# Spreading the cluster products and output transposes of the first pairs of heads over more steps, in a fused clustered-attention and channel-mix kernel

## The chip, the cores and the metric

The kernel runs on one core of a Trainium2 chip. The metric is the device time of one execution, in microseconds (us). The kernel before the change takes 252.67 us, the median of three runs (252.64 to 252.88). The profiled execution has a span of 250.9 us from its first to its last instruction, and all times read from the profile count from the start of that span.

The engines are named as in the profile: PE is the matrix engine (PEld its weight loads), DVE the vector engine, ACT the scalar engine, POOL the GpSimd engine, SP the engine that here issues most of the DMAs.

## The reference

Attention in which a query sees only the keys of its own cluster, and then a channel mix on its output:

```python
# q, k, v: (4, 8, 768, 64) f32; centroids: (8, 16, 64); d_model 512, d_ff 1024
q_assign = argmax(einsum('bhsd,hcd->bhsc', q_n, c_n), -1)      # unit-length q, centroids
k_assign = argmax(einsum('bhsd,hcd->bhsc', k_n, c_n), -1)
mask = q_assign[:, :, :, None] == k_assign[:, :, None, :]
attn = softmax(where(mask, q @ k.T / sqrt(64), -1e9))
x = (attn @ v), heads joined to (4, 768, 512)
x_prev = x shifted by one position
xk = mu_k * x + (1 - mu_k) * x_prev;  xr = mu_r * x + (1 - mu_r) * x_prev
out = sigmoid(xr @ w_r) * (relu(xk @ w_k) ** 2 @ w_v)
```

## The kernel before

The four batches of eight heads are 16 pairs of heads, numbered 0 to 15. The program is written by hand as a sequence of steps, numbered `t`; a head has six steps, a pair twelve, all heads 192. In each step the PE computes one block of scores (128 keys by 768 queries), the ACT takes its exponential, and the PE multiplies an earlier head's block with its values. The mask costs no step of its own: the 16 rows under the 64 rows of q and of k hold the one-hot code of the cluster (`aug`), so that one product of 80 rows gives score and mask at once.

```python
def scores(t):                        # one step: two matmuls and one exponential
    ...
    st = ps_st.tile([128, S], F32, name="st")          # ps_st has two buffers
    nc.tensor.matmul(st[:, 0:512], kc, a[rows, 0:512], start=True, stop=True)
    nc.tensor.matmul(st[:, 512:S], kc, a[rows, 512:S], start=True, stop=True)
    nc.scalar.activation(pt, st, AF.Exp, bias=-BIG, scale=BIG)
```

What stands between the steps prepares a coming pair: 12 transposes of its q and k on the PE (`more`, two a step for pairs 2 to 5, with a DVE copy of each four and a cast into `aug` on POOL), the product with the cluster centroids (`aff_mm`), the choice of the largest and the transposition of the one-hot code on the DVE (`aff_max`, `aff_back`), and four small DMAs that carry the code into rows 64 to 79 of `aug`.

```python
def aff_mm(n, part=0, parts=1):       # columns of one part, four products of them
    if part == 0:
        aff[n] = ps_w.tile([128, GW], F32, name="affps", tag="w")   # ps_w has two buffers
    u = slice(part * GW // parts, (part + 1) * GW // parts)         # GW = 384
    for g in range(NG):
        nc.tensor.matmul(ps[32 * g:32 * g + 32, u], cblk[...], qkT[n][:, g, u], ...)
    if part == parts - 1:
        nc.vector.transpose(t1, ps)

def aff_back(n, engs):
    nc.vector.transpose(oht, ohns[n % 2])
    for i, g in enumerate((0, 2, 1, 3)):               # the first head's two, then the second's
        engs[i % len(engs)].dma_start(augs[n % NR][g % 2][64:64 + C, ...], oht[32 * g:32 * g + C, :])
```

The output of a pair is turned by six PE transposes and one DVE copy (`xtr`), from which the two mixtures `xk` (`shift`) and `xr` (`shift_r`) are made on the DVE. The products with `w_k`, `w_r` and `w_v` of the first batch (`psk`, `psr`, `psv`) start at step 58.

The first pair goes another way, with smaller pieces (`first_trans`, `first_aff`, `first_onehot`), so that the first scores come early. The start and the steps that the change touches:

```python
nc.scalar.dma_start(cn_sb, centroids.rearrange("h c d -> (h c) d"))
nc.scalar.preload_act_table(AF.Sqrt)
load_head(0, nc.sync, nc.scalar)      # q on SP's queue, k on ACT's queue
load_head(1, nc.sync, nc.scalar)
...
cnt_ps = ...; nc.tensor.transpose(cnt_ps..., cn_sb, ident); two copies into cblk   # centroids
first_trans(0, 0); first_trans(0, 1)
use_pe(4)                             # four matmuls on zeros
first_trans(1, 0); first_aff(0, 0); first_aff(0, 1); first_trans(1, 1); first_aff(1, 0)
... first_onehot(0); first_aff(1, 1)

def first_onehot(t):                  # per head: 6 transposes of q, 6 of k, a copy of each
    for i in range(2):
        ps = ps_w.tile([128, S], BF16, name="ohps", tag="w")
        ... if i == 0: nc.vector.tensor_copy(dst, ...)
            else: nc.scalar.copy(dst, ...)
```

In a step the order on the PE is: scores, values (in every sixth step last), the step's `forced` piece, and then what `at` has put there. [...]

The softmax here doesn't subtract the row's maximum and nothing guards it: scores larger than these inputs give would overflow.

## Time and profile before

| What | Before |
|---|---|
| device time, median of 3 | 252.67 us |
| span of the profiled execution | 250.9 us |
| PE busy | 238.7 us, 95% |
| ACT busy | 189.4 us, 75% |
| DVE busy | 176.6 us, 70% |
| first score matmul starts at | 10.87 us |
| exponentials on ACT | 192, of 811 ns each |

How to read it: "busy" is the union of the times of an engine's instructions. A wait is put down to whatever ended last before it. The chain of waits follows the last instruction back in time; the timeline lists the instructions of an engine, and merges equal ones ("x4") that follow each other without a pause, with the idle time before them in square brackets. A share of the whole span hides that the kernel has several stages with different limits, so the stages are read one by one.

### The profile page before, as it was taken

To read this page: it belongs to the slowest core of one execution; us is meant where nothing else is said; L and a number is where in the kernel's file an instruction comes from. 1 tells how busy PE (TensorE), PEld (TensorE's weight loads), DVE (VectorE), ACT (ScalarE), POOL (GpSimd) and SP (SyncE) were. 2 spreads that over 40 slices of the span, in tenths; PEclk is the share of its full clock that TensorE was granted. 3 is DMA by queue.
4 is the path that set the end of the run, shared out by engine and by line. 5 is a ranking of instruction groups with operands and counts; after the bars stand their busy time and mean duration, and the time that the engine had idled before them with its cause. 6 is when DMAs were issued, how large, how long until landed. Compare 5 with 4: busy or idle time off the path is not lost.

```text
span 250.9 us, 6203 instructions
## 1 busy us (share of the span) xinstructions
PE 238.7 (95%) x2364; PEld 146.5 (58%) x2395; DVE 176.6 (70%) x340; ACT 189.4 (75%) x271; POOL 106.0 (42%) x190
## 2 busy tenths in 40 slices
PE   8999989998998999999999999999999998899994
PEld 3866766765665555555676555556566555355442
DVE  3576778698899994979967778679844427865222
ACT  5398988999897977878999877878899785146210
POOL 2968848571999737080827153712801000000000
PEclk9999999999999999999999999999999999999999
DMA  6995897879978586965959689794121121110122
GB/s 176 260 258 94 153 280 143 112 140 168 178 114 170 92 176 127 201 123 120 206 67 157 80 185 131 167 163 152 34 79 29 47 70 48 56 72 0 70 98 86
DMA packets 102462, 31.87 MB, mean 127 GB/s; under 512 B 74721, under 2 KB 98977, under 8 KB 102433
## 3 DMA queue, kind: packets, MB, share of 16 engines
q1 hardware_dynamic: 98352, 27.97, 54.3%
q0 software_dynamic: 2208, 2.62, 7.0%
q10 hardware_dynamic: 1872, 0.89, 1.3%
q8 instruction: 19, 0.31, 0.5%
q14 instruction: 11, 0.08, 0.1%
HBM read 24.15 MB, written 6.29 MB: 121 GB/s over the span
## 4 chain that ended last, share of the span: by engine, by line
PE 75%; DVE 10%; ACT 8%; issue 2%; DMA 2%; SPq 0%; DVEq 0%; ACTq 0%
PE psv L405 15%; PE st L286 13%; PE out L299 10%; PE psk L382 10%; PE psr L394 7%; ACT pt L289 7%; PE st L287 6%; PE psk L373 5%; PE affps L194 4%; DMA aug<-oht 2%; PE wps L463 2%; DVE xr L358 2%; DVE k L388 1%; DVE oht L217 1%; DVE xk L358 1%
## 5 line engine op out<-in xcount | busy, mean ns | idle before, releaser
L289 ACT ACTIVATE pt<-st 128x768 bf16<-128x768 f32 x192 | 148.2, 811 | 23.2 <-PE st L287 22.8
L175 POOL TENSOR_SCALAR aug<-qkT 64x384 bf16<-64x384 f32 x128 | 74.8, 584 | 73.1 <-DVE qkT L145 52.2
L286 PE MATMUL st<-aug 80*128 80x512 bf16 x192 | 73.1, 381 | 2.5 <-ACT pt L289 1.0
L299 PEld LDWEIGHTS <-pt 128*128 128x128 bf16 x1152 | 59.9, 97 | 26.6 <-ACT pt L289 1.4
L299 PE MATMUL out<-vt,pt 128*128 128x65 bf16 x1152 | 66.0, 193 | 0.9 <-ACT pt L289 0.8
L287 PE MATMUL st<-aug 80*128 80x256 bf16 x192 | 51.9, 270 | 0.0
L405 PE MATMUL psv<-w_v_sb,k 128*128 128x512 bf16 x173 | 44.5, 378 | 1.4 <-ACT tanh L397 0.7
L387 ACT ACTIVATE kr<-psk 128x512 bf16<-128x512 f32 x48 | 28.8, 601 | 8.1 <-PE psk L382 5.6
L388 DVE TENSOR_TENSOR k<-kr 128x512 bf16<-128x512 bf16 x48 | 22.4, 473 | 17.0 <-ACT kr L387 16.9
L382 PE MATMUL psk<-xk,w_k_sb 128*128 128x512 bf16 x113 | 30.6, 378 | 1.5 <-DVE t L198 0.8
L412 DVE SCALAR_TENSOR_TENSOR out_sb<-tanh,psv 128x512 f32<-128x512 bf16 x23 | 15.7, 682 | 21.7 <-PE psv L405 17.8
L286 PEld LDWEIGHTS <-aug 80*128 80x128 bf16 x192 | 18.7, 97 | 17.3 <-issue 7.8
L397 ACT ACTIVATE tanh<-psr 128x512 bf16<-128x512 f32 x24 | 14.4, 599 | 19.1 <-PE psr L394 18.5
L405 PEld LDWEIGHTS <-k 128*128 128x128 bf16 x184 | 16.1, 97 | 16.4 <-issue 2.4
L287 PEld LDWEIGHTS <-aug 80*128 80x128 bf16 x192 | 18.9, 98 | 9.7 <-issue 1.6
L394 PE MATMUL psr<-w_r_sb,xr 128*128 128x512 bf16 x91 | 23.7, 378 | 0.2
L145 DVE STREAM_TRANSPOSE qkT<-qk_nat 128x384 f32<-128x384 f32 x40 | 21.5, 557 | 0.0
L182 POOL CAST vt<-v_nat 128x384 bf16<-128x384 f32 x32 | 17.0, 560 | 9.5 <-DMA v_nat<-in_v_dram 8.7
L312 DVE TENSOR_TENSOR xn<-out,rs 128x384 bf16<-128x384 f32 x32 | 17.8, 558 | 1.1
L198 DVE STREAM_TRANSPOSE t<-affps 128x384 f32<-128x384 f32 x15 | 8.7, 580 | 14.0 <-PE affps L194 13.9
L382 PEld LDWEIGHTS <-w_k_sb 128*128 128x128 bf16 x128 | 11.2, 97 | 10.2 <-issue 0.9
L358 DVE SCALAR_TENSOR_TENSOR xk<-diff,mu_k_sb,xt 128x768 bf16<-128x768 bf16 x16 | 16.7, 1043 | 0.6
(65 smaller groups left out, 206.2 us busy)
## 6 DMA issues: line engine op xcount, KB each, us to landing
v_nat<-in_v_dram SPq DMA_DIRECT2D x16, 384.0 KB, 4.2
out_dram<-out_sb SPq DMA_DIRECT2D x23, 256.0 KB, 2.8
qk_nat<-in_q_dram SPq DMA_DIRECT2D x40, 96.0 KB, 4.3
qk_nat<-in_k_dram SPq DMA_DIRECT2D x40, 96.0 KB, 3.6
qk_rows<-in_q_dram SPq DMA_DIRECT2D x5, 384.0 KB, 4.4
qk_rows<-in_k_dram SPq DMA_DIRECT2D x4, 384.0 KB, 5.3
aug<-oht SPq DMA_DIRECT2D x60, 24.0 KB, 2.0
w_k_sb<-in_moe_w_k_dram POOLq DMA_DIRECT2D x4, 256.0 KB, 5.6
```

What stands on the lines that cost most here:

```text
L145: nc.vector.transpose(qkT[n][:, g, :], nat[n][:, g // 2, (g % 2) * GW:(g % 2 + 1) * GW])
L175: nc.gpsimd.tensor_scalar(augv(n, g)[0:64, par, :], in0=qkT[n][64 * par:64 * par + 64, g, :], scalar1=qk_scale, scalar2=1.0, op0=ALU.mult, ...
L286: nc.tensor.matmul(st[:, 0:512], kc, a[rows, 0:512], start=True, stop=True)
L287: nc.tensor.matmul(st[:, 512:S], kc, a[rows, 512:S], start=True, stop=True)
L289: nc.scalar.activation(pt, st, AF.Exp, bias=-BIG, scale=BIG)
L299: nc.tensor.matmul(o[:, (qc + NCH // 2) % NCH, :], pts[bh * NCH + c][:, qc * 128:(qc + 1) * 128], vts[n % NR][:, tt, 2 * (c % 3) + c // 3, ...
L358: nc.vector.scalar_tensor_tensor(out=d, in0=diff, scalar=mu[:, j:j + 1], in1=cur, op0=ALU.mult, op1=ALU.add)
L382: nc.tensor.matmul(ps, w_k_sb[:, j, ii * 128:(ii + 1) * 128], self.xk[:, j, 0:512], start=(j == 0), stop=(j == NJ - 1))
L387: nc.scalar.activation(kr, src, AF.Relu)
L388: nc.vector.tensor_tensor(dst, kr, kr, op=ALU.mult)
L394: nc.tensor.matmul(ps, self.xr[:, j, sl], w_r_sb[:, j, :], start=(j == 0), stop=(j == NJ - 1))
L405: nc.tensor.matmul(self.psvt, self.k2[:, i, sl], w_v_sb[:, i, :], start=(i == 0), stop=(i == NI - 1))
```

## The change

It does four things. The cluster products of pairs 3 to 5 are cut in four parts on four steps, where they were in two parts on two steps. The transposes of the outputs of pairs 1 and 2 are cut in two parts, on later steps that mostly hold nothing else, where they were in three parts, some on the steps of the cluster products. At the very start the loads of head 0 are issued ahead of the centroids, the transposes of head 0 stand ahead of those of the centroids, head 1 comes after the cluster products of head 0, and the last cluster product of head 1 and the transposes of pair 1 move one step later. And the steps around these are set anew: the fourth load of `w_k` goes from step 8 to step 27, and some of `shift` and `shift_r` move by some steps. What is computed stays the same. It is meant to fill the gaps between exponentials in the early stage.

```diff
+        load_head(0, nc.sync, nc.scalar)
         nc.scalar.dma_start(cn_sb, centroids.rearrange("h c d -> (h c) d"))
         nc.scalar.preload_act_table(AF.Sqrt)
-        load_head(0, nc.sync, nc.scalar)
...
+        first_trans(0, 0)
+        first_trans(0, 1)
         cnt_ps = ps_o.tile([D, H, C], F32, name="cnt_ps", tag="out2")
...
-        first_trans(0, 0)
-        first_trans(0, 1)
         use_pe(4)
-        first_trans(1, 0)
         first_aff(0, 0)
         first_aff(0, 1)
+        first_trans(1, 0)
         first_trans(1, 1)
-        first_aff(1, 0)
...
         first_onehot(0)
-        first_aff(1, 1)
+        first_aff(1, 0)
...
-            at(7 + i // 2, load_wk, i)
+            at((7, 7, 8, 27)[i], load_wk, i)
...
-            0: lambda: more(1, 0, 4, nc.vector, ps_o),
-            1: lambda: more(1, 4, 4, nc.vector, ps_o),
-            2: lambda: more(1, 8, 4, nc.vector, ps_o),
-            3: lambda: first_onehot(1),
+            0: lambda: first_aff(1, 1),
+            1: lambda: more(1, 0, 4, nc.vector, ps_o),
+            2: lambda: more(1, 4, 4, nc.vector, ps_o),
+            3: lambda: (more(1, 8, 4, nc.vector, ps_o), first_onehot(1)),
             4: lambda: aff_mm(1),
...
-            off = (6, 3, 2, 1)[n] if n < NP else 0
+            off = (6, 3, 2, 2)[n] if n < NP else 0
...
-                    a = (13, 10, 9, 8)[n]
-                    h = 1 if n == 0 else 2
+                    a = (13, 10, 9, 9)[n]
+                    h = 1 if n == 0 else 4
                     for i in range(h):
                         forced[s + a + i] = lambda n=n, i=i, h=h: aff_mm(n + 2, i, h)
                     d = a + h - 5          # aff_max on step s + 5 + d, aff_back on s + 6 + d
...
-                for i in range(3):
-                    at(e + 3 + i, xtr, n, i, 3)
+                for i in range(2):
+                    at(e + (6 if n == 1 else 7) + i, xtr, n, i, 2)
...
-            at((33, 48, 50)[n] if n < NP - 1 else x, sh)
-            at((62, 66, 70, 74)[n] if n < NP else x + 4, sh2)
+            at((33, 44, 52)[n] if n < NP - 1 else x, sh)
+            at((62, 66, 72, 75)[n] if n < NP else x + 4, sh2)
```

In the diff `s` is the first step of pair `n`, the pair that is prepared is `n + 2`, and `e` is the step after the last values of pair `n`.

## The prediction

> **What bounds the kernel now.** I read the page's busy shares first, then the busy time by stage, then the ACT's timeline of the early stages, then the waits behind its gaps.

> ```profile
> PE 238.7 (95%) x2364; PEld 146.5 (58%) x2395; DVE 176.6 (70%) x340; ACT 189.4 (75%) x271; POOL 106.0 (42%) x190
> ```

> By this line the PE is the bound. The stages say it more finely. In the next view each line is a stretch in us, its length, then busy time of PE, PEld, DVE, ACT and POOL.

> ```profile
> 0.00:10.87 10.87, 9.50 (x61) 6.59 (x62) 4.44 (x15) 4.52 (x6) 5.75 (x18) 1.00 0.74 201
> 10.87:22.00 11.13, 10.48 (x113) 7.21 (x114) 8.41 (x15) 9.94 (x13) 8.25 (x22) 1.00 0.75 203
> 22.00:32.90 10.90, 10.17 (x144) 6.97 (x141) 7.59 (x15) 9.17 (x12) 9.73 (x20) 1.00 0.87 166
> 42.00:52.00 10.00, 9.72 (x135) 6.93 (x132) 7.37 (x14) 9.36 (x13) 6.73 (x14) 1.00 0.80 126
> 72.00:82.00 10.00, 9.15 (x100) 5.88 (x100) 9.93 (x17) 8.33 (x13) 8.73 (x12) 1.00 0.76 138
> 82.00:216.00 134.00, 131.35 (x1330) 78.59 (x1351) 99.63 (x194) 109.59 (x159) 49.31 (x82) 1.00 0.61 115
> ```

> From 82 us on the PE is full: 131.35 of 134. The change does not touch that work, so whatever the early stages save or lose should reach the end unchanged. From 10.87 to about 60 us PE and ACT are nearly balanced. There the exponentials set the pace, and the time lost is the idle time in the brackets of the ACT's timeline (start, duration, what, count, idle before):

> ```profile
> 15.34 6.04 ACT L289 ACTIVATE pt<-st 128x768 bf16<-128x768 f32 x8
> 22.00 1.51 ACT L289 ACTIVATE pt<-st 128x768 bf16<-128x768 f32 x2 [0.61 <-PE st L287]
> 23.91 6.88 ACT L289 ACTIVATE pt<-st 128x768 bf16<-128x768 f32 x9 [0.40 <-PE st L287]
> 31.05 0.81 ACT L289 ACTIVATE pt<-st 128x768 bf16<-128x768 f32 x1 [0.27 <-PE st L287]
> 32.91 6.03 ACT L289 ACTIVATE pt<-st 128x768 bf16<-128x768 f32 x8 [1.04 <-PE st L287]
> 39.19 2.38 ACT L289 ACTIVATE pt<-st 128x768 bf16<-128x768 f32 x3 [0.26 <-ACT pt L289]
> 41.95 7.55 ACT L289 ACTIVATE pt<-st 128x768 bf16<-128x768 f32 x10 [0.38 <-PE st L287]
> 49.76 0.81 ACT L289 ACTIVATE pt<-st 128x768 bf16<-128x768 f32 x1 [0.27 <-PE st L287]
> 50.95 8.09 ACT L289 ACTIVATE pt<-st 128x768 bf16<-128x768 f32 x11 [0.38 <-PE st L287]
> 59.50 2.96 ACT L289 ACTIVATE pt<-st 128x768 bf16<-128x768 f32 x4 [0.47 <-PE st L287]
> ```

> Eight exponentials take 6.04 us, 0.755 a step. Counting them gives the step of each gap: 0.61 before step 12 (first step of pair 1), 0.40 before 14, 0.27 before 23, 1.04 before 24 (first of pair 2), 0.26 before 32, 0.38 before 35, 0.27 and 0.38 before 45 and 46, 0.47 before 57. Together 4.1 us. The largest is not the PE's own doing; the PE's line and SP's queue tell why:

> ```profile
> 32.33 0.38 PE L286 MATMUL st<-aug 80*128 80x512 bf16 x1 [0.73 <-DMA aug<-oht]
> 22.07 0.51 SPq L506 DMA_DIRECT2D mu_r_sb<-in_moe_mu_r_dram  x1
> 26.56 2.41 SPq L219 DMA_DIRECT2D aug<-oht  x4
> ```

> The one-hot DMAs of pair 2 took 4.3 to 5.4 us to land, where those of pair 1 took 1.8 to 3.3. Ahead of them on the same queue stands `mu_r`, 2 KB that took 9.7 us from issue, to 31.7. One more wait matters, at the start:

> ```profile
> 14.78 0.16 PEld L194 LDWEIGHTS affps<-qkT,cblk 128*32 128x32 f32 x8 [0.32 <-DVE aug L269]
> ```

> The cluster product of pair 1 waits for a DVE copy (L269) that frees its PSUM buffer.

> [...] the one-hot DMAs land right behind `mu_r`, and `mu_r` crawls while the `w_k` loads of POOL's queue run, whose last two took 6.4 and 8.1 us to land. [...]

> **Part by part.** *Cluster products.* A step without extras takes the PE 0.51 us (scores at 21.48 and 21.99), one with two transposes 0.76 (25.52 to 26.28), so the latter leaves no slack against 0.755. A half cluster product, eight matmuls of 192 columns, held the next scores back 0.47 (29.99 to 30.46), a whole one of 384 columns 0.78 (22.59 to 23.37). That is 0.059 and 0.0975 a matmul; on the same line 96 columns cost 0.039, a quarter 0.31. A step with a half takes 0.98, 0.23 over the pace, twice 0.45 a pair. With a quarter it takes 0.82, 0.07 over, four times 0.27. Of that about 0.1 is absorbed, because the scores are ready 0.1 ahead of the exponential in an even stretch (28.27 against 28.37). So pairs 3 to 5 leave 0.1 to 0.2 each where the gaps show 0.27, 0.64 and 0.65, the latter two with pieces of the output transposes (0.11 each) on the same steps. The latter now fall on steps 36 and 37 (one still shared with a quarter) and 49 and 50. Saved: 0.1 + 0.4 + 0.5 = 1.0 us.

> *Load of w_k.* The fourth goes out of the way of `mu_r` and of pair 2's code. The last two landed at 29.3 and 31.5, 2.2 apart; without the fourth the code lands about 2 us earlier, ahead of need. Saved: 1.04.

> *Step 57.* `shift` of pair 1 leaves step 48 for 44, where the DVE has room, so the copy and normalisation ahead of the last output transposes come sooner. Saved: 0.3 to 0.4.

> *The start.* It should lose. The centroids (issued at 0.74, landed 2.3 later) are issued behind k of head 0 on the ACT's queue, issued 0.5 later. With k of head 0 taking 3.8 us to land before, I put their landing near 4.3, 1.2 later. From landing to the copies of `cblk` it is 2.53 us (3.08 to 5.61), so 6.85. The first cluster products began at 6.76, held back 1.15 by transposes and filler matmuls, of which 0.33 leave that place. So they begin at 6.9 to 7.1, and the first scores come at 11.0 to 11.2: +0.2. Then step 0 holds six cluster matmuls (0.67) for four transposes (0.44): +0.24. Step 3 holds those four transposes ahead of the twelve of the one-hot code, so the ACT's copy (0.79 us, which ran without a gap) starts about 0.5 late, and the exponential of step 4 with it. And the third DVE copy of pair 1 (0.69) now stands ahead of the copy L269 for which the cluster product of pair 1 waits: +0.7. Its chain over DVE and DMA ends at step 12, which so moves from 22.0 to about 22.85. The two delays overlap. Lost: 0.85.

> *Later code.* The one-hot chains of pairs 3 to 5 end two or three steps later than before. Pair 3's landed 40.75 and 40.98 for scores at 41.98, behind two loads of rows that now share the engines with `w_k`. Pair 4's landed 50.3 for scores at 51.8. In SP's order pair 5's now stand behind six loads of `qk_nat`, which they led. Before, these margins were 1.0 us and more; with scores due about 1.5 us sooner and the code issued later they are about nothing. I allow 1.0 for waits here.

> *After 62 us.* One `shift_r` leaves the DVE's path ahead of a transposition for which the PE waited 0.79 at 77.87; but the DVE is busy 9.93 of 10 us there, so I count 0.3.

> Sum: -1.0 - 1.04 - 0.35 + 0.85 + 1.0 - 0.3 = -0.84. With the gap of step 23 likely to shrink a little more I say -1.0, so 251.6.

> **Rivals.** *One-hot DMAs become the bound.* If the code of pairs 3, 4 and 5 comes a microsecond late each time, the exponentials wait there as long as they waited in the old gaps. For it: SP's queue is nearly never empty from 29 to 50 us, and the order of pair 5. Against it: the DMAs of pair 4 took only 2 us. It would make 253 or a little more. *The start costs nothing.* If the centroids land at 3.6 rather than 4.3, the shorter PE path brings the first scores forward by 0.5 and the loss is 0.3; with no late code that makes 250.3. For it: both loads have only begun to share the engines at that time. [...] *Nothing arrives at the end.* The DVE, full from 60 to 85, gives back what came sooner. For it: 9.93 of 10. Against it: its work of these stages comes sooner too. That makes 252.3.

> **Range and chances.** The parts pull both ways, each known to some 0.4, the waits for the code to 0.8, which adds up to about 1 us. So 250.3 to 253.1. A change of 2% is 5 us, more than all gaps together and more than any delay I can name: within 2% at 0.97, faster 0.02, slower 0.01.

> **What would show it.** Right: the exponential of step 4 at 15.9 or later and of step 12 near 22.85; no gap before step 24; gaps below 0.2 where cluster products stand. Wrong: first scores before 10.7, or a wait on `aug<-oht` at step 36, 48 or 60 of over 1 us. The prediction fails as a whole if the lead at step 60 differs from the lead at the end by over a microsecond.

## The result, and the profile after

The changed kernel takes 259.88 us in the median (259.39 to 260.59), the kernel before, measured beside it, 252.65. The ratio is 1.0286 [1.0261, 1.0311]: slower by 7.2 us. The prediction was 251.6 with a range of 250.3 to 253.1.

The line is of the costliest groups, from the page of the changed kernel.

```profile
L286 PE MATMUL st<-aug 80*128 80x512 bf16 x192 | 73.6, 383 | 5.7 <-DMA aug<-oht 4.5
```

The work has hardly grown (PE busy 242.5 us for 238.7), but the score matmuls now wait 5.7 us, 4.5 of it for the one-hot code (`aug<-oht`). Next the stages, in the columns of the table shown for before; the number between POOL's busy time and the DMA share is the granted clock.

```profile
22.00:34.00 12.00, 11.59 (x164) 7.93 (x163) 8.33 (x16) 10.84 (x15) 10.64 (x21) 1.00 0.65 115
60.00:67.00 7.00, 3.34 (x47) 2.28 (x44) 5.02 (x12) 3.88 (x6) 3.56 (x7) 1.00 1.04 156
67.00:70.41 3.41, 3.19 (x20) 1.75 (x20) 0.77 (x2) 1.77 (x3) 3.12 (x5) 0.50 0.97 188
82.00:216.00 134.00, 132.64 (x1333) 79.81 (x1352) 101.95 (x197) 112.39 (x163) 53.51 (x88) 1.00 0.63 121
```

The first scores come 0.95 later, at 11.82 for 10.87. From 22 to 34 us the PE is nearly full, so the old wait before pair 2 is gone. From 60 to 67 us it is busy less than half the time, and then it runs at half the clock for 3.41 us. In the ACT's timeline, of which only the exponentials (L289) are shown, the gaps are in brackets again:

```profile
12.35 3.29 ACT L289 ACTIVATE pt<-st 128x768 bf16<-128x768 f32 x4 [0.67 <-PE st L287]
16.85 0.81 ACT L289 ACTIVATE pt<-st 128x768 bf16<-128x768 f32 x1
18.20 5.28 ACT L289 ACTIVATE pt<-st 128x768 bf16<-128x768 f32 x7 [0.54 <-PE st L287]
24.00 1.51 ACT L289 ACTIVATE pt<-st 128x768 bf16<-128x768 f32 x2 [0.52 <-PE st L287]
25.90 14.32 ACT L289 ACTIVATE pt<-st 128x768 bf16<-128x768 f32 x18 [0.40 <-PE st L287]
...
44.85 8.68 ACT L289 ACTIVATE pt<-st 128x768 bf16<-128x768 f32 x11 [0.28 <-PE st L287]
54.81 6.81 ACT L289 ACTIVATE pt<-st 128x768 bf16<-128x768 f32 x9 [1.28 <-PE st L287]
61.80 2.26 ACT L289 ACTIVATE pt<-st 128x768 bf16<-128x768 f32 x3 [0.17 <-PE st L287]
67.37 0.81 ACT L289 ACTIVATE pt<-st 128x768 bf16<-128x768 f32 x1 [3.32 <-PE st L287]
```

Counted from step 0 at 12.35, the large gaps stand before step 48 (1.28) and step 60 (3.32), the first steps of pairs 4 and 5. The one before step 48 belongs to the code of pair 4, ready at 47.76 and issued at 51.47, behind loads; it differs from run to run, for in the traces of three kernels below that are the same program up to there (`e1_code_first`, `e2_filler`, `e14_after_codes_first`) it is 0.1 to 0.3. The gap before step 24 is down to 0.1: eighteen exponentials run on from 25.90. They take 14.32. Eight took 6.04 before, of which the last is 0.81, so from start to start it is 0.747; seventeen times that and 0.81 make 13.5, and the 0.8 that is left are pauses too short to end a merged line.

I compare the two traces step by step: the offset of a step is the start of its exponential after, less that before. Step 0 +0.95, step 4 +1.51, step 12 +1.99, step 24 +0.90, step 36 +1.11, step 48 +2.42, step 56 +2.59, step 60 +5.72, step 64 +7.30, step 80 +6.97, step 191 +7.31. So 2.0 are lost by step 12, 1.1 come back at step 24, and from step 56 to step 64 4.7 are lost. From 82 us on the PE is as full as before (132.64 of 134), and the offset stays.

The next three fences show the loss at step 60: SP's queue after, SP's queue before, and the PE after.

```profile
54.60 3.71 SPq L81 DMA_DIRECT2D qk_nat<-in_q_dram  x4
58.36 3.44 SPq L81 DMA_DIRECT2D qk_nat<-in_k_dram  x2
61.90 2.41 SPq L219 DMA_DIRECT2D aug<-oht  x4
```

```profile
53.55 2.41 SPq L219 DMA_DIRECT2D aug<-oht  x4
56.05 4.17 SPq L81 DMA_DIRECT2D qk_nat<-in_q_dram  x4
```

```profile
66.70 0.39 PE L286 MATMUL st<-aug 80*128 80x512 bf16 x1 [3.38 <-DMA aug<-oht]
...
67.49 1.49 PE L382 MATMUL psk<-xk,w_k_sb 128*128 128x512 bf16 x3 [0.22 <-issue]
```

The DVE had the code of pair 5 (`oht`) ready at 58.20. SP issued it at 61.90, after six loads of `qk_nat`, and it landed at 66.33. Before, it was ready at 53.52, issued at 53.55, landed at 58.46. From issue to landing that is 4.4 us for 4.9 before, so only the issue came later. And three `psk` matmuls take 1.49 in the last line, where four took 1.03 in the trace of an experiment below: that is the half clock.

### The profile page after: what moved, and what is told of

It reads as the page before. It is cut to its first block, busy times and chain, and to the rows that moved or that the text cites. A ratio compares the mean times of both kernels' runs of the same rounds, so it can differ in the third digit from the quotient of the medians.

```text
span 258.2 us, 6302 instructions
## 1 busy us (share of the span) xinstructions
PE 242.5 (94%) x2412; PEld 148.0 (57%) x2443; DVE 177.2 (69%) x340; ACT 190.2 (74%) x271; POOL 105.6 (41%) x190
## 4 chain that ended last, share of the span: by engine, by line
PE 82%; ACT 7%; DMA 4%; DVE 4%; issue 2%; SPq 0%; ACTq 0%; DVEq 0%
PE st L286 15%; PE psv L405 15%; PE out L299 11%; PE psk L382 11%; PE psr L394 7%; PE st L287 7%; ACT pt L289 6%; PE psk L373 5%; PE affps L194 5%; DMA aug<-oht 2%; PE trps L161 2%; DMA cn_sb<-in_centroids_dram 2%; PE aff L248 1%; DVE xr L358 1%; PE xtps L327 1%
## 5 line engine op out<-in xcount | busy, mean ns | idle before, releaser
L289 ACT ACTIVATE pt<-st 128x768 bf16<-128x768 f32 x192 | 148.9, 811 | 28.3 <-PE st L287 26.9
L286 PE MATMUL st<-aug 80*128 80x512 bf16 x192 | 73.6, 383 | 5.7 <-DMA aug<-oht 4.5
L287 PE MATMUL st<-aug 80*128 80x256 bf16 x192 | 52.2, 272 | 0.0
L382 PE MATMUL psk<-xk,w_k_sb 128*128 128x512 bf16 x113 | 31.2, 385 | 0.9 <-issue 0.2
L286 PEld LDWEIGHTS <-aug 80*128 80x128 bf16 x192 | 18.8, 98 | 21.5 <-issue 6.9
L287 PEld LDWEIGHTS <-aug 80*128 80x128 bf16 x192 | 19.0, 99 | 8.5 <-issue 0.5
L182 POOL CAST vt<-v_nat 128x384 bf16<-128x384 f32 x32 | 17.6, 579 | 12.5 <-DMA v_nat<-in_v_dram 8.9
```

The lines of the kernel that those rows point to most:

```text
L382: nc.tensor.matmul(ps, w_k_sb[:, j, ii * 128:(ii + 1) * 128], self.xk[:, j, 0:512], start=(j == 0), stop=(j == NJ - 1))
```

## The experiments

The theory is that the order on SP's queue makes the wait at step 60, and that the wait makes the half clock. The first rival is that the quarters make the code itself too late; the second, that the clock falls for another reason. The start, the load of `w_k` and the quarters were also measured each alone. A ratio is against the kernel before on the same chip; offsets are those of the profiled runs. At step 0 the kernels with the old start are already -0.32 to +0.80 off, so how the offset changes within a trace says more than its height.

### The start, alone and in its two halves

`e3_start_only`, the new start in the kernel before:

```diff
+load_head(0, nc.sync, nc.scalar)                     # ahead of the centroids
 nc.scalar.dma_start(cn_sb, ...)
-load_head(0, nc.sync, nc.scalar)
 # and the new order of first_trans and first_aff, and of steps 0 to 3
```

> The kernel before with only the new start (order of the loads, order on PE, and the shift by one step of the transposes of pair 1). Theory: the start costs what the changed trace shows at step 12, 2.0 us, and nothing later gives it back: near 254.7. Rival: the delay of 2 us is absorbed by waits that follow (the 1.04 us before step 24 stands on a DMA that does not depend on it): near 253.6.

Measured: 254.29, ratio 1.0062 [1.0040, 1.0084]. The offset is +1.85 at step 12 and +1.97 at the end: the start's loss arrives in full. `e7_loads_order` changes only the order of the loads (the two `load_head` lines of the diff above), `e8_pe_order` only the order on the PE (the rest).

> The kernel before with only the loads of head 0 issued ahead of the centroids. Theory: the centroids land at 5.4 rather than 3.1, and the old order on PE puts 1.9 us of transposes and filler between them and the first cluster product, which comes at 8.7 rather than 6.8: 1.9 us slower, near 254.5. Rival: the half of the 2.0 us that shows at the first scores of the changed kernel, 253.5.

> The kernel before with only the new order on PE at the start and the shift by one step of the transposes of pair 1, the centroids still loaded first. Theory: the first scores come some 0.3 us sooner, because three transposes leave the path to the first cluster product, but steps 0 to 5 lose 1.1 us (crowded steps 0 and 3, and the copy L269 behind the third copy of pair 1): 0.7 slower, near 253.3. Rival: the loss of the start is all from the centroids' late landing, then it is 0.3 us faster, 252.3.

`e7_loads_order`: 254.80, ratio 1.0100 [1.0066, 1.0133]. The centroids land at 5.49, and the PE, which needs them first in the old order, waits. Below, the PE's line and then the filler matmuls that follow.

```profile
6.80 0.39 PE L481 MATMUL cnt_ps<-ident,cn_sb 128*64 128x128 f32 x1 [2.01 <-DVE cn_sb L479]
...
8.27 1.91 PE L463 MATMUL wps<-warm 128*128 128x512 bf16 x4
```

The work in this stretch is slow: four filler matmuls take 1.91, where the trace before shows 1.03. The kernels before and after begin so too (the first seven fillers take 3.19 in both traces). The trace's record of the clock begins only with its first change, to full, at 5.04 before and at 10.22 here, and the views print 1.00 for the time ahead of it. Here, with the wait of 2.01, full clock comes 5.18 later. `e8_pe_order`: 253.27, ratio 1.0037 [1.0017, 1.0056]; offset +1.22 at step 8, +0.80 from step 24. Both halves lose; with the PE's new order the late centroids cost less (1.97 together, against 2.75 at the end for the loads alone): in the trace of `e3_start_only` the transposes of head 0 fill the wait. Nothing in the start gains.

### The load of `w_k`, alone

`e5_wk_only`, on the kernel before:

```diff
-at(7 + i // 2, load_wk, i)
+at((7, 7, 8, 27)[i], load_wk, i)
```

> The kernel before with only the fourth load of w_k moved from step 8 to step 27. Theory: the wait of 1.04 us before step 24 goes, as in the changed trace, and nothing else moves: near 251.6. Rival: at step 27 the load takes the DMA engines from the loads of rows ahead of pair 3's code, which then comes late at step 36 and gives the microsecond back: near 252.6.

Measured: 252.08, ratio 0.9984 [0.9965, 1.0004]. The offset is -0.17 at step 12, -0.95 at steps 24 to 44, -0.47 at step 48, where pair 4's code, ready at 44.63, was issued at 48.46 behind loads, and -0.69 at the end. The gap before step 24 was worth most of its length; part is lost again to the queue. With 1 inside its interval the gain is not clear of the noise. One of its twelve runs, 277.25 us at a mean clock of 0.852, is left out of the ratio.

`e10_shifts` adds to it the changed steps of the mixtures:

```diff
-at((33, 48, 50)[n] if n < NP - 1 else x, sh)
-at((62, 66, 70, 74)[n] if n < NP else x + 4, sh2)
+at((33, 44, 52)[n] if n < NP - 1 else x, sh)
+at((62, 66, 72, 75)[n] if n < NP else x + 4, sh2)
```

> The kernel before with the load of w_k moved and the new steps of shift and shift_r, the rest as it was. Theory: 252.1 of the load alone, less the gap before step 57 (0.47), which goes because shift of pair 1 leaves the DVE's path, and less part of the 0.8 us for which the PE waits near step 75: 251.3 to 251.7. Rival, the code of pair 4 or 5 sets these steps whatever the DVE does: 252.1.

Measured: 252.16, ratio 0.9980 [0.9965, 0.9994]. The gap before step 57 is gone, as predicted, but the offset at the end is -0.5: nothing on top of the load of `w_k`.

### The quarters and the output transposes, alone

`e4_quarters_only`, on the kernel before, with the loads of pair 7 out of the way of pair 5's code:

```diff
-off = (6, 3, 2, 1)[n] if n < NP else 0
+off = (6, 3, 2, 2)[n] if n < NP else 0
-at(s + (8 if n == 2 else 12) + i // 2, load_qk, n + 4, i // 4, i % 4)
+at(s + (8 if n == 2 else 15) + i // 2, load_qk, n + 4, i // 4, i % 4)
-a = (13, 10, 9, 8)[n]
-h = 1 if n == 0 else 2
+a = (13, 10, 9, 9)[n]
+h = 1 if n == 0 else 4
-for i in range(3): at(e + 3 + i, xtr, n, i, 3)
+for i in range(2): at(e + (6 if n == 1 else 7) + i, xtr, n, i, 2)
```

> The kernel before with only the quarters of the cluster products and the output transposes on steps of their own, the loads of pair 7 kept behind the code of pair 5. Theory, the switch is paid per piece: a step with a quarter takes 0.92 us in the changed trace, not the 0.82 that was predicted, so four quarters lose 0.65 as two halves do (2 times 0.32), and the time changes by less than 0.5: 252.2 to 253.2. Rival, my prediction: 0.5 to 1.0 us faster, 251.7 to 252.2.

Measured: 257.65, ratio 1.0184 [1.0143, 1.0224]: a miss, and worth two readings. The offset is -0.31 at step 12, ahead of the first quarter, and +0.08 at step 56, so the quarters, with the output transposes on their new steps, gain nothing and rather lose a few tenths. Then step 57 comes after a gap of 2.46: the quarters end at step 48, where the DVE still makes the mixtures of pairs 1 and 2, so that `xn` begins only at 59.40. Here the PE waited for the DVE, not for a transfer, and the half clock follows all the same, from 59.65 for 6.83 us:

```profile
60.02 0.82 PE L327 MATMUL xtps<-identb,xn 128*128 128x128 bf16 x6 [1.67 <-DVE xn L312]
```

The whole change avoids this by its other steps of `shift`; so this experiment is no measure of the quarters' later effects. Why they gain nothing up to step 56 stands in the changed kernel's PE timeline, from the scores of one step to those of the next, with a quarter between:

```profile
32.29 0.39 PE L286 MATMUL st<-aug 80*128 80x512 bf16 x1
...
32.90 0.37 PE L194 MATMUL affps<-qkT,cblk 128*32 128x96 f32 x8
33.21 0.39 PE L286 MATMUL st<-aug 80*128 80x512 bf16 x1
```

From scores to scores it is 0.92 (32.29 to 33.21). The quarter holds the next scores back 0.31 (32.90 to 33.21), as predicted, and the rest of the step should take 0.51; 0.10 is missing. The last values matmul begins at 32.78, and its neighbours follow each other every 0.03, but the cluster product begins 0.12 after it. That pause comes once for each piece. Over the pace of 0.747, a step with a quarter (0.917) loses 0.17, four times 0.68; a step with a half takes 1.077 (29.38 to 30.46 in the trace before) and loses 0.33, twice 0.66.

### The order on SP's queue, in the kernel before

`e6_loads_first` changes nothing but the steps at which the loads of pair 7 are issued, so that six of them stand ahead of pair 5's code, as in the changed kernel:

```diff
-at(s + (8 if n == 2 else 12) + i // 2, load_qk, n + 4, i // 4, i % 4)
+at(s + (8 if n == 2 else 9) + i // 2, load_qk, n + 4, i // 4, i % 4)
```

> The kernel before with only the loads of pair 7 moved three steps earlier, so that six of them stand ahead of the code of pair 5 on SP's queue, as in the changed kernel. Before, SP stood idle from 51.0 to 53.5, so that six loads of 0.55 to 1 us each would end near 56 to 57, the code, ready at 53.5, would land near 60 to 61, and step 60 needs it at 60.9. Theory, order alone is only part of it (the code is also ready 4.7 us later in the changed kernel): 0 to 1 us slower, 252.6 to 253.6. Rival, order alone makes the whole loss: 256 or more.

Measured: 257.77, ratio 1.0210 [1.0174, 1.0245]. The view of SP's queue, of the PE, and of the stretch after:

```profile
51.55 3.36 SPq L81 DMA_DIRECT2D qk_nat<-in_q_dram  x4
54.95 3.44 SPq L81 DMA_DIRECT2D qk_nat<-in_k_dram  x2
58.49 3.39 SPq L219 DMA_DIRECT2D aug<-oht  x4
```

```profile
63.54 0.61 PE L286 MATMUL st<-aug 80*128 80x512 bf16 x1 [2.35 <-DMA aug<-oht]
```

```profile
62.63:69.46 6.83, 5.70 (x34) 3.44 (x36) 2.50 (x5) 3.03 (x4) 6.05 (x11) 0.50 0.75 132
```

The code was ready at 53.50, issued at 58.49, 5.0 later, and landed at 63.31, 4.8 after that. The offset is -0.01 at step 56 and +5.84 from step 76. No quarter, no new start: the order alone costs 5.1 us, by a wait of 2.35 and 6.83 us at half clock. My small expectation fell, the rival in it held.

### The order mended in the changed kernel

`e1_code_first` moves the same loads behind pair 5's code; `e9_pair5_old` gets the same by taking pair 5's product back to halves on its old steps:

```diff
 # e1_code_first
-at(s + (8 if n == 2 else 12) + i // 2, load_qk, n + 4, i // 4, i % 4)
+at(s + (8 if n == 2 else 15) + i // 2, load_qk, n + 4, i // 4, i % 4)
 # e9_pair5_old
-off = (6, 3, 2, 2)[n]; a = (13, 10, 9, 9)[n]; h = 1 if n == 0 else 4
+off = (6, 3, 2, 1)[n]; a = (13, 10, 9, 8)[n]; h = (1, 4, 4, 2)[n]
```

> The changed kernel with one thing undone: on SP's queue the one-hot code of pair 5 stands again ahead of the loads of pair 7 (those move from steps 48 to 51 to steps 51 to 54). Theory, queue order: the code was ready at 58.2 us and was issued only at 61.9, behind six loads; issued at once it lands near 61, the wait at step 60 (3.3 us) and the half clock after it (1.7 us) go, and about 5 us of the 7.2 come back: near 254.7. Rival, the DMA engines are simply full at that time, or the code is late because its chain on the DVE is late: the code lands late in any order, and the time stays above 258.

> The changed kernel with the cluster product of pair 5 alone back in two halves on its old steps (44 and 45), so that its code is chosen on step 46 and issued on step 47, ahead of the loads of pair 7, which keep their steps. Theory: the code of pair 5, [...] makes everything beyond the start; with it at its old place neither step 60 nor step 72 waits, the PE keeps its clock, and what is left is the start (2.0) less the wait at step 24 (1.0): 253 to 254. Rival, the late codes of pairs 3 and 4 would do the same one pair on: 255 or more.

`e1_code_first`: 256.45, ratio 1.0148 [1.0108, 1.0189]. `e9_pair5_old`: 255.33, ratio 1.0124 [1.0088, 1.0160]. In both traces the wait at step 60 is gone (offsets +0.92 and +1.37 there). `e1_code_first`, which keeps the late quarters, rules out the first rival: the code is in time if it is issued when it is ready (57.02 and 57.05). But both stay above what was expected of them, and both traces have a new wait at step 72, for pair 6's code, which now stands behind the loads of pair 8. The profiled run of `e9_pair5_old` is its slowest, 257.51; the other three took 254.89 to 255.39, with a mean clock of 1.00. `e1_code_first`:

```profile
78.16 0.38 PE L286 MATMUL st<-aug 80*128 80x512 bf16 x1 [2.17 <-DMA aug<-oht]
...
79.57 0.62 PE L286 MATMUL st<-aug 80*128 80x512 bf16 x1
```

The same score matmul takes 0.38 at 78.16 and 0.62 at 79.57: the clock falls to half from 79.51, 1.35 us after the wait has ended, for 3.41 us.

`e14_after_codes_first` mends both orders:

```diff
 # e1_code_first, and
-at(s + (12 if n == NP else 9) + i, load_qk, n + 4, i // 4, i % 4)
+at(s + (14 if n == NP else 9) + i, load_qk, n + 4, i // 4, i % 4)
```

> The changed kernel with the order on SP's queue mended for two pairs: the code of pair 5 ahead of the loads of pair 7, and two of the loads of pair 8 behind the code of pair 6. Theory, order on the queue is the whole loss beyond the start, and the wait only moved one pair on when pair 5 alone was mended: now no wait at 60 nor at 72, no half clock, and the start (2.0) less step 24 (1.0) is left: 253 to 254. Rival, the DMA engines cannot carry loads and codes in time once the codes are ready later, whatever their order: the wait moves on again, 255 or more.

Measured: 254.82 (254.09 to 256.97), ratio 1.0118 [1.0077, 1.0160], between the theory and its rival. No half clock, offset +1.36 at step 60. The excess falls from 2.9% to 1.2%: two numbers in the issue of loads give back some 4.2 of the 7.2 us. Of what is left, 1.1 stand in the trace at step 24 already: the start, less the wait before step 24. A little of the rival stays: pair 6's code was issued at once (73.02) but landed only at 77.01, 4.0 later, where it took 2.7 before, and the PE waits 0.85 at step 72.

`e15_codes_first_old_start` puts the old start into that.

> The same with the start as before the change: all of the change but its start, with the codes first. Theory: the start costs 2.0 us here too, so 2.0 less than the kernel it is compared with, 251 to 252. Rival: waits elsewhere hide the difference, or a code is late again: 253 or more.

Measured: 255.61, ratio 1.0121 [1.0085, 1.0158], a miss. At step 24 it is 1.7 ahead of the kernel with the new start (-0.64 for +1.10), near the expected 2.0; at step 96 1.0 of that is left (+0.48 for +1.44), as step 36 alone loses 0.75, where pair 3's code comes late. Then steps 110 and 114 lose 1.0 and 1.25. The DVE's line tells of what:

```profile
118.78 0.36 DVE L349 TENSOR_TENSOR diff<-xt 128x384 bf16<-128x384 bf16 x1 [2.17 <-DMA xt<-xn]
```

The output of a later pair is turned by a DMA, which SP issued at 115.60 behind three loads that took it 3.04 us. It looks like the same cause on another transfer, but this is read from the trace only; no run tests it.

### The half clock

`e2_filler` leaves the wait at step 60 of the changed kernel and fills it with fifteen matmuls on zeros:

```diff
+if n == NP - 1:
+    at(59, use_pe, 15)
```

> The changed kernel with 15 matmuls on zeros (about 0.215 us each, 3.2 us) on PE at the end of step 59, just where it waits 3.4 us for the code of pair 5. They add nothing to the result and fill only the wait. Theory, half clock: the PE ran at half clock for 3.4 us after the wait because it had been idle, and a PE that was busy keeps its clock: 1.7 us less, near 258.2, with the wait itself still there. Rival, the half clock has another cause, or the lag of step 61 to 64 is work that the wait piled up: no change or slower by the filler, 259.9 or more.

Measured: 257.78, ratio 1.0210 [1.0166, 1.0253]. From the PE's timeline:

```profile
61.89 3.40 PE L463 MATMUL wps<-warm 128*128 128x512 bf16 x15
65.98 0.39 PE L286 MATMUL st<-aug 80*128 80x512 bf16 x1 [0.69 <-DMA aug<-oht]
...
66.31 1.03 PE L382 MATMUL psk<-xk,w_k_sb 128*128 128x512 bf16 x4
```

The exponentials still wait there, 3.99 us, but the clock stays at 1.00, and from step 60 to 64 the offset stays (+4.92, +4.93), where the changed kernel went from +5.72 to +7.30. All four runs have a mean clock of 0.999 or 1.00, those of the changed kernel 0.987 to 0.993. Work that computes nothing makes the kernel about 2 us faster: 257.78 for 259.88. Between the two traces it is 2.25 at the end, of which 0.80 was there at step 60 already, because this trace has only 0.3 of the gap at step 48. So here the idle PE brings the half clock, 3.41 us of it after an idle time of 3.38 and none where fillers are in the wait, and the second rival falls.

### What remains of the change

On the kernel before, with the new load of `w_k`: `e11_code4_first` moves the loads of pair 6 behind pair 4's code, `e12_combined` adds to that the new steps of the mixtures and the output transposes in two parts, `e13_codes_first` adds to that pair 8's loads behind pair 6's code, and `e16_no_xtr` takes the output transposes back to three parts. Halves and the old start stay in all.

```diff
 # e11_code4_first
-at(s + (8 if n == 2 else 12) + i // 2, load_qk, n + 4, i // 4, i % 4)
+at(s + (10 if n == 2 else 12) + i // 2, load_qk, n + 4, i // 4, i % 4)
 # e13_codes_first
-at(s + (12 if n == NP else 9) + i, load_qk, n + 4, i // 4, i % 4)
+at(s + (14 if n == NP else 9) + i, load_qk, n + 4, i // 4, i % 4)
 # e12_combined and e13_codes_first have it, e16_no_xtr doesn't
-for i in range(3): at(e + 3 + i, xtr, n, i, 3)
+for i in range(2): at(e + (6 if n == 1 else 7) + i, xtr, n, i, 2)
```

> The kernel before with the load of w_k moved, and the loads of pair 6 two steps later, so that two of the eight stand behind the code of pair 4 on SP's queue. With the load of w_k moved alone, this code was ready at 44.6, issued at 48.5 behind all eight, and step 48 had a gap of 0.42. Theory, order on the queue: the gap goes, 251.6. Rival: the code of pair 5 or the loads of pair 6 then come late and take it back, 252.1 or more.

> The kernel before with all that seems to help: the load of w_k moved, the loads of pair 6 behind the code of pair 4, the new steps of shift and shift_r, and the output transposes in two parts on steps of their own; the start and the cluster products as before. Theory: the gains add, 0.5 for the load, 0.4 for the code of pair 4, 0.5 at step 57 and 0.1 to 0.2 for the output transposes: 250.8 to 251.3. Rival: each gain is given back at the next code that lands late: 252.

> The version that combined what seems to help, and lost 2.9 us to a wait at step 72, with one more order set right: two of the loads of pair 8 behind the code of pair 6, which was ready at 70.5 and issued at 73.6. Theory: the wait and the half clock after it go, and the gains of the early stages (0.9 us at step 60) reach the end: 250.3 to 251.5. Rival, the engines are full and the wait moves on once more: 252 or more.

> The last one with the output transposes in three parts on their old steps. Theory: they cost the early stages 0.1 to 0.2 us, which the DVE or the queue can hide: within 0.3 us of the version with two parts. Rival: the shorter early stages only make a code late, and this one is faster than that.

| Kernel | us | ratio | from the trace |
|---|---|---|---|
| `e11_code4_first` | 252.26 | 0.9986 [0.9971, 1.0002] | code lands at 49.31, gap at step 48 gone |
| `e12_combined` | 252.53 | 0.9997 [0.9974, 1.0021] | -0.91 at step 60; waits 2.10 at step 72, half clock for 3.41 us (a run of 254.48) |
| `e13_codes_first` | 252.12 | 0.9987 [0.9972, 1.0003] | no wait at step 72, -1.59 at step 60, -1.2 to -1.4 at the end (a run of 251.26) |
| `e16_no_xtr` | 251.76 | 0.9983 [0.9966, 0.9999] | -1.58 at step 60, -0.3 at the end (a run of 252.40) |

Of the fourteen runs of `e12_combined` four have a mean clock of 0.985 to 0.993 and take 254.38 to 256.23, the profiled one among them; the ten others have 0.997 to 1.00 and take 251.16 to 253.64. So the half clock of its trace is not the usual case. The first three kernels missed the times expected of them and leave 1 inside their intervals. `e16_no_xtr` is the best in the median, by 0.36 us over `e13_codes_first`, within the spread of both. In the medians, what comes 1.6 us sooner at step 60 is mostly given back later.

## Why the prediction was wrong

*Later code* is the step that failed: "I allow 1.0 for waits here", and in the first rival "253 or a little more". Measured: 1.3 at step 48, 3.3 at step 60, and 1.6 by the half clock up to step 64. The prediction saw the order ("pair 5's now stand behind six loads of `qk_nat`"), but has no term for the time that the loads ahead take to issue: SP needed 7.2 us for six of them (54.60 to 61.80), and the code stood ready for 3.7 us before it was issued. That is 1.2 us a load on average, at a DMA share of 1.06 from 54.60 to 61.80, and it was the wait. That the order suffices is shown by `e6_loads_first` (+5.1 us) and `e14_after_codes_first` (4.2 back).

The *half clock* is in no term of the sum. Nothing in the profile before shows it in the middle of the kernel; the longest wait of the PE after its first scores there is 0.79. In the trace of the changed kernel it makes the 1.6 up to step 64, and `e2_filler` puts it at about 2 us between the medians. The profiled run is a mild one: its mean clock, 0.993, fits 3.41 us at half (an estimate: half of 3.41 in 258.2), the 0.987 of the other three fits 6.83.

*The start*: mechanism right, size off: 2.0 for 0.85. The term is the landing of the centroids: I put 4.3, it was 5.39: issued 0.5 later, behind `k` and beside `q` of head 0, they took 4.1 to land, not 2.3. With the centroids first, `e8_pe_order` has +0.99 at step 12, near the 0.85. Step 4 began at 16.85 ("15.9 or later" held), step 12 at 24.00, not 22.85.

*Cluster products*: nothing for the 1.0 predicted. Of the gaps counted for them, the 0.26 before step 32 was not theirs: pair 4's first half stood on step 33, and the gap is still there (0.26 at 40.48). A quarter costs 0.31 as I had it, but each piece also costs a pause of 0.10 on the PE: a step takes 0.92, not 0.82. My 0.98 for a step with a half missed the pause too (1.08), so four pieces pay it four times and two pieces twice. The pace of 0.755 counts the last exponential's whole length; from start to start it is 0.747.

*Load of w_k*: right, -0.78 between steps 12 and 24 for -1.04 (`e5_wk_only`), partly lost again at step 48. *Step 57*: right, 0.17 for 0.47. *After 62 us*: the wait of 0.79 on the PE is gone and the offset falls by 0.95 from step 72 (+7.92) to step 80, but from step 64 (+7.30) to the end (+7.31) nothing is gained.

*Right if* named no gap before step 24 and gaps below 0.2 at the cluster products: 0.1 is left of the first, 0.28 stands before step 37. *Wrong if* named a wait over 1 us at step 48 or 60, and both came. The lead at step 60 and the lead at the end differ by 1.6 (+5.72, +7.31): the half clock, which comes after the exponential of step 60. By the prediction's own words it failed as a whole. Of the rivals, the one with the late code had the right place and the wrong size; the one with a free start fell; and that a lead is given back was not tried by the changed kernel, which never had one, but the last kernels speak for it in part: of leads of 1.6 at step 60, 1.4 and 0.3 reached the end in the two traces, and 0.3 and 0.4 by the ratios.

Left open: which idle time brings the half clock. Waits of 1.67, 1.75, 2.10, 2.17, 2.35 and 3.38 us did; one of 0.98 in `e3_start_only` and the one of 1.11 at step 48 of the changed kernel did not; between these nothing was tried. Open too is why the kernels with all codes first lose their lead: both go from -2.5 at step 80 to -1.5 at step 84, and `e16_no_xtr` loses 1.0 more at steps 114 and 162.

## What to carry to other kernels

In this kernel small urgent transfers had to stand ahead of bulk loads on their queue at the time they were ready: behind six loads the code of pair 5 was issued 3.7 us late. So when a producer moves by two steps, look at what the queue issues in those two steps, and count the issue time of each load in the busy stage (here 1.2 us). A wait of the PE of some 2 us cost a third more than its length in one trace, and more than twice as much in another (2.9 us for 2.17 in `e1_code_first`, 5.8 for 2.35 in `e6_loads_first`), because matmuls at half clock came with it, for 3.41 and 6.83 us. Cutting work into more pieces gains only if the switch (here 0.10 us a piece) costs less than the slack that each piece finds.

## What the runs showed of the hardware

The half-clock stretches were 3.41 us (the changed kernel, `e1_code_first`, `e9_pair5_old`, `e12_combined`) or 6.83 us (`e4_quarters_only` and `e6_loads_first`). 1.67 us without a matmul was enough in `e4_quarters_only`, 2.17 in `e1_code_first`. In `e1_code_first` the fall came 1.35 us after the PE had started again, in the changed kernel 0.30. So here waits of 1.7 us are already long ones.

```profile
76.10:79.51 3.41, 1.35 (x15) 1.15 (x16) 2.10 (x5) 0.81 (x1) 3.06 (x6) 1.00 0.42 72
```

The PE was busy 1.35 us of it, and 0.30 to 2.00 us in the 3.41 us ahead of the five other falls in mid-kernel (0.30 in the changed kernel, 63.59 to 67.00; 2.00 in `e4_quarters_only`, 56.24 to 59.65). A stretch with 2.17 in `e3_start_only` brought no fall, but one with 1.61 near the end of `e4_quarters_only` (250.80 to 254.21) brought none either, so no fixed limit comes out. The half clock lasted a second 3.41 us where the wait reached into the first (`e4_quarters_only` and `e6_loads_first`, busy 3.04 and 2.28 of 3.41); in the four others the PE was busy 3.19 to 3.41 there.

The PE pauses about 0.10 when it goes from the values' matmuls to a cluster product (`affps`), once for each piece: in the changed kernel the product begins 0.12 after the last values matmul (32.78 to 32.90), where the values' own follow each other every 0.03. The two differ in weight columns (128 and 32) and in type (bf16 and f32); which of these makes the pause was not tried.
